# Scan bursts, block turns and weight sums at other places of a Mamba-2 scan with an ELU feed-forward

## The chip, the cores and the metric

The kernel runs on one NeuronCore of a Trainium2 chip. The metric is the device time of one execution in microseconds, as the median of six runs. The profile is one execution, taken by the hardware profiler.

## The reference

The inputs are x [4, 8, 768, 32], a decay a [4, 8, 768], B and C [4, 8, 768, 16], and two weight matrices w_in [256, 2048] and w_out [2048, 256] that come as 64-bit floats. A state-space scan runs for each batch and head over the sequence; its result y, with the heads side by side, is the input of a feed-forward block with an ELU.

```python
for c in range(nc):                      # chunks of the sequence
    cum = np.cumsum(log_a[:, :, sl], axis=-1)
    L = np.exp(cum[..., :, None] - cum[..., None, :]) * causal
    M = np.einsum('bhin,bhjn->bhij', Cc, Bc) * L
    y[:, :, sl] = M @ xc + np.einsum('bhin,bhnd->bhid', Cc, state) * np.exp(cum)[..., None]
    state = decay_full * state + sum_j (B_j * decay_from_j) x_j
...
x = y.transpose(0, 2, 1, 3).reshape(3072, 256)
h = x @ w_in
g = np.where(h > 0, h, np.exp(np.minimum(h, 0)) - 1)
out = g @ w_out                          # [3072, 256]
```

## The kernel before

The 3072 tokens are cut into 12 blocks of 256 (n = 0 to 11); a block is one of the three parts of one batch's sequence, with all eight heads. Within a block the scan works on chunks of 64 tokens. The order of the instructions on every engine is written out by hand in one program; the loops at the end of the function decide what follows what. All DMAs of the part concerned here are issued by SyncE (SP), in the order of the program.

**The scan of a block** has these steps:
- `load_bc(n)` (L106) and `load_x(n)` (L132) fetch B, C and x. For n > 5 B and C are fetched in a layout "of squares" (L121) for VectorE's transposes, and B once more by tokens (L113, tile b_tok). For n up to 5 B and C come by tokens alone (L129). `spread_cum` and `spread_exp` fetch the sums of the decays.
- The turn of B and C: blocks up to 5 use `turn(n)` (L383): four TensorE transposes into two PSUM tiles (L389), a copy to SBUF by ScalarE (L393) and the masked C by VectorE (L396), then `turn_exp(n)` (L400, L404). From block 6 on `turn_part(n, part)` is used: parts 0 and 1 are one VectorE transpose each (L413), part 2 the masked C (L421), part 3 the `turn_exp` (L404).
- `scaled(n)` (L374, on GpSimd) makes B times a decay, tile sc; `decay` makes L on ScalarE and GpSimd.
- `scores` (L501), `sums` (L531), `across` (L576) and `inside` (L595) are bursts of many small TensorE products: `scores` 32 for each block, `sums` 24 or 32, `across` up to 32 and `inside` 64. `weigh` (L510) multiplies the scores by L on VectorE, and `states` (L548, L553) carries the state; its tiles Sx are read by `across`. The end of a block is `inside(across(n), n)`, whose results are copied to yT.

**The feed-forward block** takes two forms. Blocks 0 to 3 use plain products: `l1(n, i)` (L625) makes a slice h, `elu` (L638, L645, L647) makes g, `l2(n, i)` (L746) adds to the output. Blocks 4 to 11 are handled in pairs (n, n+1) with seven products in place of eight at both matrices. `front`, `mid` and `back` (products at L697, sums by VectorE at L714, L722 and L730) make h for a pair; `second(n)` is a generator whose every step issues two products (L807) for the output of the pair. It lags by two blocks: while n = 4 is in `front`, `second(2)` runs. Its sums of g are made on GpSimd (L762, L774).

In a pair `front` writes the PSUM tile c2, `front_sums` (L714) reads both halves of it on VectorE into the tile u_sum, and the second product of `mid` then adds to a half of c2 that `front_sums` has read.

The sums of the weights for the seven products are made in place by `sum_weights` (four operations at L673), for w_out on VectorE and for w_in on GpSimd, one of eight slices at a time. `more_sums(i)` does slice i of both, and one sum of g on VectorE (L774). In the kernel before, slices 0 to 5 are made while n = 3, and slices 6 and 7 are spread over the first steps of n = 4 (`left`).

**The order around the change.** For n = 2 and 3 there is a loop of eight steps i: `l2(n - 2, i)`, `l1(n, i)`, the elu, and `scan_ahead(n, i)`, which holds the scan steps of blocks that come later. For n = 4, 6, 8, 10 there is a loop of 16 half steps k. An even k has `front`, an elu and four steps of `second` (`l2s`); an odd k has `mid`, `back`, two elus and three steps of `second`. The scan of the next pair m = n + 2 is laid between them: `scores(m, m + 1)` at k = 9, `sums` at k = 10, `states` at k = 11. The table `ends` says at which step of which n the end of a pair of blocks (across, inside, and `sum_y` on GpSimd) is issued.

PSUM is one pool of seven tiles in rotation (ps_h, ps_g, ps_st, ps_y, ps_tb, ps_tc and every second ps_o), and one tile apart.

`idle_product(k)` (L229) is a product of zeros with k times 128 columns, issued three times at the start: twice ahead of the first data, once ahead of `weigh(0, 0)`.

Of the kernel before, what the change touches and what calls it, by code (L numbers as in the profile page):

```python
# [16 lines left out]
P = 128  # L17
# [11 lines left out]
def kernel(  # L29
# [76 lines left out]
    def load_bc(n, c_queue=nc.sync):  # L106
        b, g = place(n)
        st.setdefault(n, {})["bc"] = raw.tile([P, 2, 2, NH, N], F32, tag="bc", name="bc", bufs=2)
        if n > 5:
            st[n]["b"] = raw.tile([P, 2, NH, N], F32, tag="b", name="b_tok", bufs=2)  # L110
            for u in range(2):
                sl = slice((2 * g + u) * P, (2 * g + u + 1) * P)
                nc.sync.dma_start(  # L113
                    out=st[n]["b"][:, u], in_=B[b, :, sl, :].rearrange("h s n -> s h n"))


            squares = st[n]["bc"].rearrange("p k u h n -> p k (u h n)").rearrange(
                "p k (m r) -> p k m r", m=2)
            for k, src in enumerate((B, C)):
                for m in range(2):  # L120
                    nc.sync.dma_start(  # L121
                        out=squares[:, k, m],
                        in_=src[b, m:NH:2, g * BLK:(g + 1) * BLK, :].rearrange(
                            "q (c t) n -> q c (t n)", t=8))
            return
        for u in range(2):
            sl = slice((2 * g + u) * P, (2 * g + u + 1) * P)
            for k, src in enumerate((B, C)):
                (nc.sync, c_queue)[k].dma_start(  # L129
                    out=st[n]["bc"][:, k, u], in_=src[b, :, sl, :].rearrange("h s n -> s h n"))  # L130
# [98 lines left out]

    def idle_product(k):  # L230

        nc.tensor.matmul(  # L232
            out=ps_idle[:, 0:k], lhsT=idle, rhs=idle.unsqueeze(1).to_broadcast([P, k, P]),
            start=True, stop=True)

    idle_product(4)
    idle_product(3)
# [136 lines left out]
    def scaled(n, eng):  # L374

        s = st[n]
        s["sc"] = sc = att.tile([P, 2, NH, N], F32, tag="sc", name="sc", bufs=2)
        factor = eb0[:, :, NH * n:NH * (n + 1)] if n < 2 else eb[:, :, rows_of(n)]
        eng.tensor_tensor(
            out=sc, in0=s["b"] if n > 5 else s["bc"][:, 0],  # L380
            in1=factor.unsqueeze(3).to_broadcast([P, 2, NH, N]), op=ALU.mult)

    def turn(n):  # L383
# [16 lines left out]
    def turn_exp(n, eng=nc.vector):  # L400

        s = st[n]
        s["cts"] = att.tile([P, 2, P], F32, tag="cts", name="cts", bufs=2)
        eng.tensor_tensor(out=s["cts"], in0=s.pop("ct"), in1=s["ec"], op=ALU.mult)  # L404
# [258 lines left out]
    def sum_weights(eng, a, s, i):  # L663
        for step in weight_steps(eng, a, s, i):
            step()
# [337 lines left out]
            elu()  # L1003


    ends = {(3, 13): (4, 5), (4, 13): (6, 7), (6, 13): (8, 9), (8, 12): (10, 11)}

    def end_of_two(n, step):
        ns = ends.get((n, step))
# [9 lines left out]
    def scan_ahead(n, i):  # L1019


        m = n + 2 + n % 2
        if 4 < m < NP and n % 2 == 1 and i in (4, 5):
            spread_cum(m + i - 4)
        m = n + 2 - n % 2
        if 4 <= m < NP and n % 2 == 0:
            if i < 2:
                if m == 4:
                    load_bc(m + i)
                spread_exp(m + i)  # L1030
            if i == 2:
                if m == 4:
                    spread_cum(5)
                load_x(m)
                load_x(m + 1)
            for k in (i,) if m == 4 else (i, i + 1) if i % 2 == 0 else ():
                if k >= 2:
                    decay(m + k // 6, (k - 2) % 4)
            if m == 4 and i in (5, 7):
                turn(m + i // 7)  # L1040
                turn_exp(m + i // 7)
        if n % 2 == 1 and i in (1, 3) and n + 3 + i // 2 < NP:
            load_bc(n + 3 + i // 2)
        if n == 3 and i > 3 and i < 7:
            turn_part(6, i - 4)
        if 4 <= m < NP and n % 2 == 1:
            if i == 0:
                scaled(m, nc.gpsimd)
                scaled(m + 1, nc.gpsimd)
            for k in (i,) if m == 4 else (i, i + 1) if i % 2 == 0 else ():  # L1050
                if k < 2:
                    decay(m + 1, k + 2)
            if i == 2 and m == 4:
                scores(m, m + 1)
                sums(m, m + 1)
                for q in range(4):
                    weigh(m, q)
                    weigh(m + 1, q)
                states(m)
                states(m + 1)  # L1060
# [21 lines left out]
    for n in (2, 3):  # L1082
        for i in range(8):
            l2(n - 2, i)
            if todo < len(pieces):
                w_take(todo, nc.vector)
            end_of_two(n, 2 * i)
            l1(n, i)
            if todo < len(pieces):
                w_give(todo)  # L1090
                w_load(todo + 6)
                todo += 1
            while lag:
                elu()
            if n == 2:
                if i < 2:
                    decay(3, 2 * i)
                    decay(3, 2 * i + 1)
                if i == 1:
                    scaled(3, nc.gpsimd)  # L1100
                    turn(3)
                    turn_exp(3)
                if i == 2:
                    scores(3)
                    for q in range(4):
                        weigh(3, q)
                if i == 4:
                    sums(3)
                    states(3)
                if i == 6:  # L1110
                    inside(across(3), 3)
            else:
                if i == 0:
                    s_in[:], s_out[:] = weight_sums(), weight_sums()
                elif i < 7:
                    more_sums(i - 1)
            scan_ahead(n, i)
            end_of_two(n, 2 * i + 1)
    sum_t2(2, 0)
    left = (step for i in (6, 7) for step in weight_steps(nc.vector, a_out, s_out, i))  # L1120

    for n in range(4, NP, 2):
        m = n + 2 if n + 2 < NP else None
        steps = second(n - 2)

        def l2s(count):
            for _ in range(count):
                next(steps)

        def next_elu():  # L1130
            if lag:
                at = lag[0][:2]
                elu()
                if at[0] % 2:
                    sum_t1(at[0] - 1, at[1])

        for k in range(16):
            i = k // 2
            if k % 2 == 0:
                if m and i == 5:  # L1140
                    l2s(4)
                    next_elu()
                    weigh_two(m, 1)
                    sums(m, m + 1)
                    front(n, i)
                    weigh_two(m, 2)
                    front_sums(n, i)
                    weigh_two(m, 3)
                else:
                    front(n, i)  # L1150
                    front_sums(n, i)
                    next_elu()
                    l2s(2)
                    end_of_two(n, k)
                    l2s(2)
            elif m and i == 5:
                l2s(1)
                mid(n, i)
                begin_elu()
                states(m)  # L1160
                l2s(2)
                back(n, i)
                next_elu()
                states(m + 1)
                begin_elu()
            else:
                mid(n, i)
                if i == 0 and n > 4:
                    store(n - 4, 0)
                    store(n - 4, 1)  # L1170
                begin_elu()
                turn_step(n, k, False)
                l2s(2)
                back(n, i)
                next_elu()
                begin_elu()
                turn_step(n, k, True)
                if n == 4 and i < 4:
                    for _ in range(2):
                        next(left)()  # L1180
                    if i < 2:
                        sum_weights(nc.gpsimd, a_in, s_in, 6 + i)
                        sum_t1(2, 6 + i)
                l2s(1)
            if m:
                scan_ahead(n + k // 8, k % 8)
                if k == 9:
                    scores(m, m + 1)
                    weigh_two(m, 0)
                if k % 2:  # L1190
                    end_of_two(n, k)
        for _ in steps:
            pass
# [44 lines left out]
```

## Time and profile before

| what | value |
|---|---|
| median of 6 runs | 362.88 us (362.57 to 364.58) |
| profiled execution, its own time | 364.58 us |
| its span, first to last instruction | 362.9 us |
| mean granted TensorE clock | 0.994 |
| TensorE matmuls busy | 353.6 us, 97% |
| VectorE, ScalarE, GpSimd busy | 66%, 55%, 64% |
| DMA moved | 26.09 MB in 85,845 packets |

The stretches of the span, by TensorE's timeline: 0 to 53.8 us blocks 0 and 1 with the conversion of the weights; 53.8 to 85.5 us n = 2; 85.5 to 117.7 us n = 3; from 117.7 us the pairs n = 4, 6, 8 and 10; from 334 us the last pair's second product alone. A busy time of TensorE includes overlaps of matmuls that follow each other; the difference of two starts in the timeline tells what one costs. A gap is shown with what ended it; "issue" stands where the profile shows nothing that the engine waited for.

### The profile page before, as it was taken

Reading aid. Unit: us, or ns where it says so; the run is one execution under the profiler, and the core shown is the slowest. Engines: PE = TensorE matmul, PEld = TensorE weight load, DVE = VectorE, ACT = ScalarE, POOL = GpSimd, SP = SyncE. Lnnn points to the kernel's source line nnn. Section 1 sums busy time; section 2 is a strip of 40 time slices with the busy share of each in tenths; the row PEclk is TensorE's granted clock in tenths of the full one; section 3 lists DMA queues with packets and bytes.
Section 4 is the critical chain, followed back from the end, with each engine's and each line's share of the span. In section 5 each row is a group of like instructions: output and inputs, shape, how many; then the busy total and the mean of one; then the engine's idle time right before and its main releaser. Section 6 shows DMA issues by size and latency. Waiting matters only on the chain.

```text
span 362.9 us, 9921 instructions
## 1 busy us (share of the span) xinstructions
PE 353.6 (97%) x3954; PEld 316.0 (87%) x3954; DVE 240.4 (66%) x495; ACT 201.0 (55%) x493; POOL 231.9 (64%) x368
## 2 busy tenths in 40 slices
PE   8899999999999999999999999999989999999995
PEld 5578878888888998989999989999979999999995
DVE  3989987982699778674777574777563456556212
ACT  4758969767435676545576545576534443535000
POOL 4553543673557997879386969386966445455983
PEclk9999999999999999999999999999998999999999
DMA  8977999552350500146500146500000100000001
GB/s 147 223 191 144 239 312 176 85 94 45 71 119 15 106 0 3 18 97 139 101 0 2 18 100 135 103 3 0 2 2 4 58 2 1 0 2 31 30 2 58
DMA packets 85845, 26.09 MB, mean 72 GB/s; under 512 B 63848, under 2 KB 81704, under 8 KB 85800
## 3 DMA queue, kind: packets, MB, share of 16 engines
q1 hardware_dynamic: 83624, 25.27, 31.8%
q8 instruction: 31, 0.51, 0.6%
q10 hardware_dynamic: 2176, 0.20, 0.5%
q14 instruction: 14, 0.11, 0.1%
HBM read 22.12 MB, written 3.34 MB: 70 GB/s over the span
## 4 chain that ended last, share of the span: by engine, by line
PE 83%; DVE 5%; POOL 4%; ACT 2%; issue 2%; DMA 2%; SPq 1%; POOLq 0%
PE ps_o L807 32%; PE ps_h L697 25%; PE ps_h L625 10%; PE ps_o L746 8%; PE ps_y L595 2%; DMA w<-in_moe_w_in_dram 2%; POOL g L762 2%; SPq L129 1%; PE ps_g L501 1%; PE ps_y L576 1%; PE ps_st L531 1%; DVE mag L200 1%; PE ps_idle L232 1%; DVE sgn L192 1%; POOL g L774 1%
## 5 line engine op out<-in xcount | busy, mean ns | idle before, releaser
L638 ACT ACTIVATE e<-ps_h 128x512 f32<-128x512 f32 x96 | 57.1, 594 | 92.2 <-DVE ps_h L722 45.4
L807 PEld LDWEIGHTS ps_o<-w_out,g 128*128 128x128 f32 x640 | 80.3, 192 | 3.3 <-issue 0.5
L807 PE MATMUL ps_o<-w_out,g 128*128 128x128 f32 x640 | 81.4, 275 | 0.0
L647 DVE SCALAR_TENSOR_TENSOR g<-e,ps_h 128x512 f32<-128x512 f32 x96 | 65.1, 679 | 15.8 <-ACT e L645 15.3
L625 PE MATMUL ps_h<-yT,w_in 128*128 128x256 f32 x256 | 60.7, 383 | 2.2 <-ACT w_in L181 1.1
L645 ACT ACTIVATE e<-e 128x512 f32<-128x512 f32 x96 | 60.9, 635 | 2.0
L774 POOL TENSOR_TENSOR g<-g 128x256 f32<-128x256 f32 x34 | 25.2, 742 | 55.4 <-DVE g L647 55.4
L625 PEld LDWEIGHTS ps_h<-yT,w_in 128*128 128x128 f32 x256 | 47.7, 190 | 10.5 <-POOL w_in L217 3.2
L807 PE MATMUL ps_o<-w_sum,g 128*128 128x128 f32 x320 | 43.8, 279 | 0.0
L807 PEld LDWEIGHTS ps_o<-w_sum,g 128*128 128x128 f32 x320 | 42.0, 195 | 1.5
L481 ACT ACTIVATE L<-L,ncum 128x64 f32<-128x64 f32 x160 | 41.0, 337 | 0.0
L697 PE MATMUL ps_h<-y_sum,w_sum 128*128 128x256 f32 x128 | 39.0, 387 | 0.5 <-DVE u_sum L714 0.5
L697 PE MATMUL ps_h<-yT,w_in 128*128 128x256 f32 x128 | 39.2, 388 | 0.0
L697 PE MATMUL ps_h<-y_sum,w_in 128*128 128x256 f32 x128 | 38.1, 380 | 0.0
L730 DVE TENSOR_TENSOR ps_h<-ps_h,u_sum 128x512 f32<-128x512 f32 x32 | 22.4, 699 | 23.6 <-PE ps_h L697 23.5
L486 POOL TENSOR_SCALAR_AFFINE_SELECT L<-L 64x512 f32<-64x512 f32 x40 | 27.8, 696 | 13.1 <-ACT L L481 11.8
L722 DVE TENSOR_TENSOR ps_h<-ps_h,u_sum 128x256 f32<-128x256 f32 x32 | 13.8, 432 | 30.1 <-PE ps_h L697 29.7
L714 DVE TENSOR_TENSOR u_sum<-ps_h,u_sum 128x512 f32<-128x512 f32 x32 | 22.0, 688 | 13.3 <-PE ps_h L697 7.9
L746 PE MATMUL ps_o<-w_out,g 128*128 128x256 f32 x128 | 30.8, 383 | 0.0
L762 POOL TENSOR_TENSOR t<-g 128x256 f32<-128x256 f32 x40 | 29.4, 766 | 0.3
L762 POOL TENSOR_TENSOR g<-g,t 128x256 f32<-128x256 f32 x40 | 28.8, 752 | 0.2
L697 PEld LDWEIGHTS ps_h<-y_sum,w_sum 128*128 128x128 f32 x128 | 24.2, 192 | 5.5 <-DVE u_sum L714 2.3
(111 smaller groups left out, 539.7 us busy)
## 6 DMA issues: line engine op xcount, KB each, us to landing
L<-flat SPq DMA_DIRECT2D x20, 256.0 KB, 6.1
w<-in_moe_w_in_dram SPq DMA_DIRECT2D x8, 512.0 KB
w<-in_moe_w_out_dram SPq DMA_DIRECT2D x8, 512.0 KB, 9.9
xr<-in_x_dram SPq DMA_DIRECT2D x24, 128.0 KB, 2.8
out_dram<-c_sum SPq DMA_DIRECT2D x10, 256.0 KB
bc<-in_B_dram SPq DMA_DIRECT2D x24, 64.0 KB, 5.9
bc<-in_C_dram SPq DMA_DIRECT2D x22, 64.0 KB
ec<-flat_exp SPq DMA_DIRECT2D x9, 128.0 KB
```

The source lines that it names most:

```text
L481: nc.scalar.activation(L[:, h, u], L[:, h, u], ACT.Exp, bias=ncum[:, u, row:row + 1])
L486: nc.gpsimd.affine_select(out=part, in_=part, pattern=[[0, 4], [0, 2], [1, Q]], compare_op=ALU.is_ge, fill=0.0, base=0, channel_multiplier=-1)
L625: nc.tensor.matmul(out=ps[:, j], lhsT=w_in[:, k, m * P:(m + 1) * P], rhs=yT[n // 2][:, k, n % 2].rearrange("p u i -> p (u i)"), start=(k = ...
L638: nc.scalar.activation(begun[0], lag[0][2], ACT.Relu, scale=-1.0)
L645: nc.scalar.activation(e, e, ACT.Exp, scale=-1.0)
L647: nc.vector.scalar_tensor_tensor(out=g_of[n, i], in0=e, scalar=1.0, in1=ps, op0=ALU.subtract, op1=ALU.max)
L697: nc.tensor.matmul(out=out, lhsT=lhsT, rhs=rhs, start=first, stop=True, skip_group_check=True)
L730: nc.vector.tensor_tensor(out=c2, in0=c2, in1=u[:, 0:2], op=ALU.add)
L746: nc.tensor.matmul(out=o_of[n][:, ts], lhsT=g_of[n, j][:, m % 2, ts * P:(ts + 1) * P], rhs=w_out[:, m], start=(m == 0 and ts == 0), stop=( ...
L762: nc.gpsimd.tensor_tensor(out=out, in0=in0, in1=in1, op=ALU.subtract)
L774: eng.tensor_tensor(out=b12, in0=b12, in1=b11, op=ALU.subtract)
L807: nc.tensor.matmul(out=ps[:, ts], lhsT=b[:, ts * P:(ts + 1) * P], rhs=a[:, i], start=(i == chunk[0] and ts == 0), stop=(i == chunk[-1]), s ...
```

## The change

- Blocks 4 and 5 are loaded in squares and by tokens, as blocks from 6 on were, and turned by `turn_part` in place of `turn`. The parts lie in the steps i = 3 to 7 of n = 2, and i = 0, 2 and 3 of n = 3.
- Slice 6 of the weight sums is made by `more_sums(6)` at the last step of n = 3, and its sum of g goes to VectorE with it. `left` holds slice 7 alone, one VectorE operation in each of four steps.
- The end of the blocks 10 and 11 is issued at k = 13 of n = 8 in place of k = 12.
- In n = 4, 6 and 8 one step of `second` is taken from the end of k = 9, ahead of `scores`, and put ahead of `mid` at k = 11.
- `idle_product(k)` issues k products of 128 columns in place of one with k times 128.

```diff
     def load_bc(n, c_queue=nc.sync):
...
-        if n > 5:
+        if n > 3:
             st[n]["b"] = raw.tile([P, 2, NH, N], F32, tag="b", name="b_tok", bufs=2)
...
     def idle_product(k):
-        nc.tensor.matmul(
-            out=ps_idle[:, 0:k], lhsT=idle, rhs=idle.unsqueeze(1).to_broadcast([P, k, P]),
-            start=True, stop=True)
+        for j in range(k):
+            nc.tensor.matmul(out=ps_idle[:, j], lhsT=idle, rhs=idle, start=True, stop=True)
...
-            out=sc, in0=s["b"] if n > 5 else s["bc"][:, 0],
+            out=sc, in0=s["b"] if n > 3 else s["bc"][:, 0],
...
-    ends = {(3, 13): (4, 5), (4, 13): (6, 7), (6, 13): (8, 9), (8, 12): (10, 11)}
+    ends = {(3, 13): (4, 5), (4, 13): (6, 7), (6, 13): (8, 9), (8, 13): (10, 11)}
...
     # scan_ahead
-            if m == 4 and i in (5, 7):
-                turn(m + i // 7)
-                turn_exp(m + i // 7)
+            if m == 4 and i > 2:
+                turn_part(m + i // 6, i % 3)
...
-        if n == 3 and i > 3 and i < 7:
+        if n == 3 and i == 0:
+            turn_part(5, 2)
+        if n == 3 and i in (2, 3):
+            turn_part(i + 2, 3)
+        if n == 3 and i in (4, 5, 6):
             turn_part(6, i - 4)
...
     # n = 3, step i
                 if i == 0:
                     s_in[:], s_out[:] = weight_sums(), weight_sums()
-                elif i < 7:
+                else:
                     more_sums(i - 1)
...
-    left = (step for i in (6, 7) for step in weight_steps(nc.vector, a_out, s_out, i))
+    left = weight_steps(nc.vector, a_out, s_out, 7)
...
     # n = 4, 6, 8, 10, half step k
             elif m and i == 5:
-                l2s(1)
+                l2s(2)
                 mid(n, i)
...
                 if n == 4 and i < 4:
-                    for _ in range(2):
-                        next(left)()
-                    if i < 2:
-                        sum_weights(nc.gpsimd, a_in, s_in, 6 + i)
-                        sum_t1(2, 6 + i)
-                l2s(1)
+                    next(left)()
+                    if i == 0:
+                        sum_weights(nc.gpsimd, a_in, s_in, 7)
+                        sum_t1(2, 7)
+                if not m or i != 4:
+                    l2s(1)
```

## The prediction

> **What bounds the kernel now.** First the page's busy line, then TensorE's timeline and its list of waits, then VectorE's timeline where the change puts work.
>
> ```profile
> PE 353.6 (97%) x3954; PEld 316.0 (87%) x3954; DVE 240.4 (66%) x495; ACT 201.0 (55%) x493; POOL 231.9 (64%) x368
> q8 instruction: 31, 0.51, 0.6%
> ```
>
> TensorE is the bound: from 28 us on it is dense, so each matmul removed or stall added there moves the end one for one, unless it meets one of the few gaps. The second line becomes important: 0.51 MB in 31 packets are 16 KB each, TensorE's own instructions.
>
> ```profile
> 52.70 1.24 PE L625 MATMUL ps_h<-yT,w_in 128*128 128x256 f32 x5 [0.24 <-issue]
> 76.33 0.38 PE L389 MATMUL ps_tb<-ident,bc 128*128 128x128 f32 x2
> 76.55 0.38 PE L389 MATMUL ps_tc<-ident,bc 128*128 128x128 f32 x2
> 76.77 1.89 PE L746 MATMUL ps_o<-w_out,g 128*128 128x256 f32 x8
> 121.18 0.59 PE L697 MATMUL ps_h<-y_sum,w_sum 128*128 128x256 f32 x2
> 140.30 0.70 PE L697 MATMUL ps_h<-y_sum,w_sum 128*128 128x256 f32 x2 [0.52 <-DVE u_sum L714]
> 268.55 1.24 PE L576 MATMUL ps_y<-cts,Sx 32*64 32x64 f32 x64
> 269.71 0.79 PE L595 MATMUL ps_y<-M,xr 64*32 64x64 f32 x56
> 272.00 0.96 PE L595 MATMUL ps_y<-M,xr 64*32 64x64 f32 x72 [1.50 <-issue]
> ```
>
> Columns are start, duration, operation, idle before. See: four transposes take 0.44 us of the stream (76.33 to 76.77); one wait of 0.52 us for VectorE's u_sum; and two gaps with releaser "issue", at 52.7 and in the middle of the scan burst of blocks 10 and 11 at 270.5.
>
> **The gaps are instruction fetches.** Numbering TensorE's records (loads, matmuls, semaphore events) in order of start, the work resumes after the gaps at records 1473 and 6593: 5,120 apart, 20 times 256. The Trainium skill, "Runtime: NRT & Kernel Launch", section "Instruction fetch mechanics", says that instructions come in 16 KiB blocks of 256, the next fetched while the present one runs, at a cost mostly hidden. The packet size and the 5,120 agree; "hidden" does not hold here. Block starts are thus records 193+256k. In the packet list the two fetches start 1.79 and 1.37 us after TensorE enters a block without lead (52.70, 272.00), and the next block runs 2.5 to 2.7 us after the packet starts (50.16 to 52.70; 269.29 to 272.00). Under heavy DMA load, early, the first part is longer: 3.0 us after 9.09, 4.3 after 23.09, 3.9 after 46.24. A scan burst eats a block in 1.5 us, a plain stretch in 14 or more. Taking 2.6 us to arrival, the slack at every block start works out as positive except at the two gaps; the smallest others are 0.85 us at record 449, 0.96 at 961 and 1.93 at 5569.
>
> **The clock.**
>
> ```profile
> 271.00:272.00 1.00, 0.00 (x0) 0.00 (x0) 0.00 (x0) 0.00 (x0) 0.92 (x2) 1.00 0.00 0
> 274.00:275.00 1.00, 1.00 (x6) 0.91 (x6) 0.00 (x0) 0.29 (x1) 0.57 (x1) 0.50 0.00 0
> ```
>
> The third value from the end is the granted clock: after the gap it is half for 3.4 us. "TensorE: Matmul & The Clock Gate", Part 1, describes half rate after low activity, in windows of 3,413 ns; the trace agrees. The loss is 1.7 us. The profiled execution took 364.58 us (span 362.9 and 1.7 around it), the median is 362.88: exactly this window less. So I add up against 362.88, and assume the burst's stall itself is in every run.
>
> **VectorE ahead of the first pair.**
>
> ```profile
> 116.72 0.94 DVE L774 TENSOR_TENSOR g<-g 128x256 f32<-128x256 f32 x1
> 117.59 1.21 DVE L421 TENSOR_TENSOR ctm<-bct,hmask 128x512 f32<-128x512 f32 x1
> 119.16 0.69 DVE L647 SCALAR_TENSOR_TENSOR g<-e,ps_h 128x512 f32<-128x512 f32 x1 [0.36 <-PE ps_h L697]
> 119.76 0.69 DVE L714 TENSOR_TENSOR u_sum<-ps_h,u_sum 128x512 f32<-128x512 f32 x1
> ```
>
> VectorE has no idle from 99.85 to 118.8; the first pair's u_sum ends at 120.45, and TensorE's second product of mid(4,0), which overwrites what u_sum reads, starts at 121.18: slack 0.73 us.
>
> **Part by part.**
>
> 1. *Blocks 4 and 5 turned by VectorE.* TensorE loses two times four transposes: 0.44 + 0.43 us, -0.9. ScalarE loses two copies (0.35 each), off the path. VectorE loses 2 x (0.68+0.42), gains four 32-row transposes (L413, 0.64 each, 0.49 from start to start), two masks (L421, 0.7 to 1.2) and two cts (L404, 0.43). The first two transposes enter 62 to 80 us, where VectorE is dense and w_out pieces 14 and 15 end on GpSimd 0.5 and 1.5 us before l2 takes them: 0 to +0.5. I take 0, since I expect TensorE later there (part 4). PSUM gains four free tiles. SP issues six DMAs instead of four per block, two at 0.58 each more; it idles from 62.7 to 66.7, and the load is used 4 us or more after its landing (median 5.9 after issue). B of block 6 now waits for sc(4) at 89.7 instead of leaving at 85.2; its first use is at 110: nothing.
>
> 2. *more_sums(6) in the last step of block 3.* GpSimd's four L673 (2.1 us) now precede t2, which TensorE needs at 128.2 and which would end at 123.6: nothing. VectorE's four L673 and one L774 stand ahead of u_sum of the first pair. Such groups take 1.85, 2.27, 2.28, 2.54 and 2.92 us in the trace, mean 2.4; the spread is VectorE and GpSimd excluding each other ("SBUF — State Buffer", section "SBUF: two separate sides": a lock held for the whole instruction; the L673 of 0.26 and 0.76 us agree). The two cts put in at block 3 cost 2 x 0.34 less 0.36 of idle: +0.3. So u_sum ends at 120.45 + 2.7 = 123.15 against 121.18: **+2.0** (1.4 to 2.7). In return each step in n = 4 has one sum fewer, u_sum at 139.57 comes some 0.6 us sooner, and the 0.52 wait goes: -0.5.
>
> 3. *Last burst from step 12 to 13.* At 268.55 the burst waited for Sx, made until 269.02, and then for its block. A whole burst takes 2.42 us elsewhere (218.35 to 220.77) and 4.41 here: **-2.0** if both waits go. In its new place some 57 records later the Sx are old and the entered block was asked for some 6 us before. The block after it begins about 46 records past the burst, which take some 3.1 us, against 2.8 until it arrives: bounds 0 to +0.7, I take 0. y_sum has two steps left, as after the bursts of the other pairs. The l2 step moved past scores, three times, makes scores 0.44 us earlier and gives mid more cover (0.14 us wait at 155.6 each); but sums then meets a PSUM tile freed at 152.26 by L647: 0, bounds ±0.4.
>
> 4. *Idle products as single matmuls.* Each fp32 matmul is two loads and two matmuls; ten instead of three add 28 records (20 before record 134). Their own time is set by columns: 128-column matmuls in L807 follow each other in 0.111 us, hardly more than wide ones: 0. But every later record moves 28 on against the block starts, until the turns take 16 back.
>    - Record 449 falls into the end of inside(0), reached at 12.05; asked for at 8.8, fetched at 11.85, there at 14.45. The first l1 starts at 15.0, not 13.27. It absorbs its own wait for w_in; about 0.9 is left at 23.
>    - Record 961 is now the head of l1 of block 1, due at 28.05. Asked for while sums(1) runs at 23.9, fetched 4.3 later, there at 30.8 (30.0 without the delay before). From here TensorE is dense: +2.5 (1.9 to 3.0).
>    - Record 1473 falls 22 records inside the burst of block 2: 1.5 us of stall instead of 0.4: +0.9 (-0.4 to +1.2).
>
>    Together **+3.4**, bounds -0.4 (no stall appears, the old 0.4 goes) to +4.2.
>
> Sum: -0.9 + 2.0 - 0.5 - 2.0 + 3.4 = +2.0, hence 364.9 us.
>
> **Rivals.**
> - *Fetches keep ahead (faster).* If the early fetches do not depend on the 28 records as I think, because the blocks are asked for earlier than I infer, part 4 is about 0. For it: early latencies are read with unknown lead. Against it: only two starts have no slack, and just these stall. Sum -1.4: 361.5. The sign turns where part 4 costs less than 1.4 us.
> - *u_sum not late.* If VectorE catches up before 117 us, part 2 gives -0.5 alone: 362.9. Against it: no idle for 19 us.
> - *A cold window too.* An early stall after a burst resembles the one at 270.5 and may halve the clock for 3.4 us: +1.7, 366.6.
> - *The burst moved in vain.* If it straddles another late block, its 2.0 stays: 366.9.
>
> **How the numbers follow.** Main case 0.50 (own range 363.6 to 366.3), fetches ahead 0.25 (360.6 to 362.6), u_sum not late 0.11 (362.0 to 364), the last two 0.14 (366 to 368). About 0.3%, or 1.1 us, is what can be told from no change: under 361.8 lies most of the second case, 0.22; between, parts of three cases, 0.19; over 364.0, 0.59. Range 360.9 to 367.2.
>
> **What would show it.** Right: "issue" gaps near 12, 28 and 54 us; l1 of block 1 at about 30.5; a wait of about 2 us for L714 at mid(4,0); none at the last burst, clock full after it. Wrong: the dense stretch starting at 28, or no wait at mid(4,0).

## The result, and the profile after

| what | before | after |
|---|---|---|
| median, measured side by side | 363.23 us (72 runs, 361.5 to 366.28) | 363.92 us (35 runs, 361.29 to 366.84) |
| ratio of after to before | | 1.0013, 95% interval 0.9999 to 1.0026 |
| profiled execution, its own time | 364.58 us | 365.76 us |
| its span | 362.9 us | 364.0 us |
| its mean granted TensorE clock | 0.994 | 0.986 |

The change made no difference that can be told from none. The forecast was slower by 2.0 us; the measured 364 us lie inside its range. The two profiles end 1.1 us apart, but they are not alike: matmul by matmul the changed kernel lies 4.2 us behind after the first stall, 6.2 us behind after the second (at 123 us of before), and wins most of it back at the last burst. Lines past L233 have a number one lower than before.

The page's busy line and the line of the granted clock (40 slices of the span, tenths of full speed):

```profile
PE 353.5 (97%) x3960; PEld 318.7 (88%) x3960; DVE 241.8 (66%) x500; ACT 200.5 (55%) x491; POOL 231.3 (64%) x367
PEclk9789999999999989999999999999999999999999
```

TensorE is as busy as before, with six matmuls more. The clock dips in the slices 2, 3 and 15 (of 9.1 us each). TensorE's longest waits (total, times, longest, in us):

```profile
PE ps_y L594 <- issue: 2.8, 1, 2.8
PE ps_h L696 <- DVE u_sum L713: 2.5, 1, 2.5
```

These are the two new waits that the prediction named. TensorE's timeline (start, duration, operation, idle before and what ended it) places them. First two lines of before, then the kernel after:

```profile
11.12 1.01 PE L595 MATMUL ps_y<-M,xr 64*32 64x64 f32 x64
28.08 10.63 PE L625 MATMUL ps_h<-yT,w_in 128*128 128x256 f32 x48
```

```profile
11.23 0.99 PE L594 MATMUL ps_y<-M,xr 64*32 64x64 f32 x60
15.02 0.42 PE L594 MATMUL ps_y<-M,xr 64*32 64x64 f32 x4 [2.79 <-issue]
...
31.44 4.80 PE L624 MATMUL ps_h<-yT,w_in 128*128 128x256 f32 x21
...
53.53 1.22 PE L594 MATMUL ps_y<-M,xr 64*32 64x64 f32 x64
...
122.67 0.60 PE L696 MATMUL ps_h<-yT,w_in 128*128 128x256 f32 x2
125.79 0.67 PE L696 MATMUL ps_h<-y_sum,w_sum 128*128 128x256 f32 x2 [2.53 <-DVE u_sum L713]
...
278.12 1.51 PE L594 MATMUL ps_y<-M,xr 64*32 64x64 f32 x128
```

The burst `inside(0)` stops four matmuls before its end; the work resumes at record 449. The long l1 of block 1 starts at 31.44, against 28.08 before. In the burst of block 2 at 53.53, record 1473 starts 0.34 us after the record before it (0.13 us of it idle). At `mid(4,0)` the second product waits 2.53 us. The last burst, which took 4.41 us, has no gap: `inside` of blocks 10 and 11 is one piece of 1.51 us. The 0.52 us wait that stood at 140.30 is gone.

The windows of the trace (the granted clock is the third value from the end) show what follows each of the two stalls:

```profile
16.00:17.00 1.00, 1.00 (x4) 0.82 (x3) 0.56 (x2) 1.00 (x3) 0.50 (x1) 0.50 0.82 276
21.00:22.00 1.00, 1.00 (x19) 0.85 (x19) 0.62 (x2) 0.33 (x2) 0.34 (x1) 1.00 0.47 122
127.00:128.00 1.00, 1.00 (x6) 1.00 (x5) 0.48 (x1) 0.97 (x2) 1.00 (x2) 0.50 0.00 0
130.00:131.00 1.00, 1.00 (x7) 0.92 (x6) 1.00 (x3) 0.59 (x2) 1.00 (x2) 1.00 0.00 0
```

Half rate holds from 14.0 to 20.8 us (two windows of 3.413 us on end) and from 126.6 to 130.0 (one). Each such window can cost up to 1.7 us. In before's profile there is one, after the gap in the last burst.

**The same split over all runs.** Every run lists its mean granted clock, and one window of 3.41 us at half rate lowers it by about 0.005. So the clock of a run tells how many windows it had. Of 35 runs of after 3 had none (361.4 us in the median), 7 had one (362.8), 19 had two or nearly so (364.0) and 6 three (365.6). Of the 107 runs of the kernel before that were made beside the experiments, 78 had none (some 362.9 us) and 29 had one or, twice, two. The clock tells only how many windows a run had; where they lie is seen in the profiled run alone. **At full clock, then, the change is a gain of about 1.4 us (three runs); the windows of half clock, which in the profile follow its two new stalls, take it back.**

### The profile page after: what moved, and what is told of

Read it like the earlier page. It is cut to its first block, busy times and chain, and to the rows that moved or that the text cites. A ratio compares the mean times of both kernels' runs of the same rounds, so it can differ in the third digit from the quotient of the medians.

```text
span 364.0 us, 9939 instructions
## 1 busy us (share of the span) xinstructions
PE 353.5 (97%) x3960; PEld 318.7 (88%) x3960; DVE 241.8 (66%) x500; ACT 200.5 (55%) x491; POOL 231.3 (64%) x367
## 4 chain that ended last, share of the span: by engine, by line
PE 95%; DVE 2%; issue 1%; POOL 0%; POOLq 0%
PE ps_o L806 34%; PE ps_h L696 27%; PE ps_h L624 16%; PE ps_o L745 8%; PE ps_y L594 3%; PE ps_g L500 2%; PE ps_y L575 2%; PE ps_st L530 1%; PE ps_idle L233 1%; PE ps_x L451 1%; PE ps_x L440 0%; PE ps_x L459 0%; POOL w_in L217 0%; DVE w_sum L672 0%; PE ps_tb L388 0%
## 5 line engine op out<-in xcount | busy, mean ns | idle before, releaser
L773 POOL TENSOR_TENSOR g<-g 128x256 f32<-128x256 f32 x33 | 24.0, 728 | 57.7 <-DVE g L646 57.6
L624 PEld LDWEIGHTS ps_h<-yT,w_in 128*128 128x128 f32 x256 | 49.1, 194 | 7.8 <-POOL w_in L217 0.2
L806 PE MATMUL ps_o<-w_sum,g 128*128 128x128 f32 x320 | 42.9, 275 | 0.0
L806 PEld LDWEIGHTS ps_o<-w_sum,g 128*128 128x128 f32 x320 | 41.1, 192 | 1.2
L696 PE MATMUL ps_h<-y_sum,w_sum 128*128 128x256 f32 x128 | 38.2, 380 | 2.5 <-DVE u_sum L713 2.5
L485 POOL TENSOR_SCALAR_AFFINE_SELECT L<-L 64x512 f32<-64x512 f32 x40 | 28.9, 722 | 11.1 <-ACT L L480 9.7
```

The source lines that it names most:

```text
L485: nc.gpsimd.affine_select(out=part, in_=part, pattern=[[0, 4], [0, 2], [1, Q]], compare_op=ALU.is_ge, fill=0.0, base=0, channel_multiplier=-1)
L624: nc.tensor.matmul(out=ps[:, j], lhsT=w_in[:, k, m * P:(m + 1) * P], rhs=yT[n // 2][:, k, n % 2].rearrange("p u i -> p (u i)"), start=(k = ...
L696: nc.tensor.matmul(out=out, lhsT=lhsT, rhs=rhs, start=first, stop=True, skip_group_check=True)
L773: eng.tensor_tensor(out=b12, in0=b12, in1=b11, op=ALU.subtract)
L806: nc.tensor.matmul(out=ps[:, ts], lhsT=b[:, ts * P:(ts + 1) * P], rhs=a[:, i], start=(i == chunk[0] and ts == 0), stop=(i == chunk[-1]), s ...
```

## The experiments

All times are medians, with the ratio to the kernel before on the same chip. "No window" means runs at a mean clock of 0.997 or more.

Theory: TensorE's instructions come in blocks of 256, and a scan burst that reaches a block start too early stalls; VectorE's queue makes u_sum late; a stall draws half clock. Rivals: the split costs by its own matmuls; GpSimd's sums are what is late; the parts do as the prediction sized them, without windows.

### The idle split alone

```diff
-        nc.tensor.matmul(
-            out=ps_idle[:, 0:k], lhsT=idle, rhs=idle.unsqueeze(1).to_broadcast([P, k, P]),
-            start=True, stop=True)
+        for j in range(k):
+            nc.tensor.matmul(out=ps_idle[:, j], lhsT=idle, rhs=idle, start=True, stop=True)
```

> The kernel before with the idle products alone split into single matmuls (28 more TensorE records, nothing else). Fetch theory: record 449 falls into the end of inside(0), so a gap of releaser issue of 2 to 3 us stands near 12 us, l1 of block 0 starts at about 15 instead of 13.3, and what is left of it at l1 of block 1 (28.1 us before) is 1 to 3 us; the burst of blocks 10 and 11 still stalls, since 28 records move block start 6593 from record 243 of the burst to record 215, still inside. Time +1.0 to +2.5 us. Rival (the split itself costs nothing and the order of the stream is all the same): no gap at 12 us, time within 0.5 us.

Measured: 364.42 us (360.43 to 366.43), ratio 1.0003 (0.9974 to 1.0033). TensorE's timeline:

```profile
15.08 0.43 PE L594 MATMUL ps_y<-M,xr 64*32 64x64 f32 x4 [3.07 <-issue]
...
55.58 0.33 PE L594 MATMUL ps_y<-M,xr 64*32 64x64 f32 x11 [1.46 <-issue]
...
273.60 1.51 PE L594 MATMUL ps_y<-M,xr 64*32 64x64 f32 x128
```

The split makes two stalls, at records 449 and 1473, and removes a third, against my forecast. The block start 6593 still lies in the last burst, at 274.02, as expected, but its block is not late: the packet came at 267.71, 6.3 us before it was needed, in place of 2.7 us in before (269.29 for 272.00). The block that TensorE runs meanwhile is entered 28 records sooner, 3.5 us ahead of `across` in place of 0.9. With this stall gone the median is that of before, and not the 1.0 to 2.5 us more that I expected. Twelve of 14 runs have windows (364.7 us); the two without took 360.4 and 361.1.

### The change without the idle split

The edit is the one above, undone in the changed kernel.

> The changed kernel with the idle products as one matmul each, as before. Fetch theory: no issue gap near 12 us, l1 of block 1 back at about 28.1 us, the later stall of about 2.5 us at mid(4,0) stays. Time 1 to 2.5 us under the changed kernel, so 362 or less, and faster than before by some 1 us. Rival (the early stall is absorbed before TensorE becomes dense): no change against the changed kernel.

Measured: 362.77 us, 1.2 us under the changed kernel, ratio 0.9973 (0.9955 to 0.9991); without a window 361.4 (10 runs), with one or more 363.1 (12 runs).

```profile
12.90 2.49 PE L625 MATMUL ps_h<-yT,w_in 128*128 128x256 f32 x8 [1.13 <-POOL w_in L217]
...
123.53 0.67 PE L697 MATMUL ps_h<-y_sum,w_sum 128*128 128x256 f32 x2 [2.52 <-DVE u_sum L714]
```

No fetch gap at 12 us, only the first l1's wait for its weights; the wait for u_sum stays.

### The change without the moved weight sums

```diff
-                else:
+                elif i < 7:
                     more_sums(i - 1)
...
-    left = weight_steps(nc.vector, a_out, s_out, 7)
+    left = (step for i in (6, 7) for step in weight_steps(nc.vector, a_out, s_out, i))
...
                 if n == 4 and i < 4:
-                    next(left)()
-                    if i == 0:
-                        sum_weights(nc.gpsimd, a_in, s_in, 7)
-                        sum_t1(2, 7)
+                    for _ in range(2):
+                        next(left)()
+                    if i < 2:
+                        sum_weights(nc.gpsimd, a_in, s_in, 6 + i)
+                        sum_t1(2, 6 + i)
```

> The changed kernel with the weight sums of slice 6 back in the first steps of n = 4 (left, as before). Theory of VectorE's queue: the wait of 2.5 us for u_sum at mid(4,0) goes, a wait of 0 to 0.5 us at mid(4,3) comes back; the gap at 12 us stays. Time 1.5 to 2.5 us under the changed kernel, more where the stall also cost a cold clock window. Rival (the wait is due to the two cts of blocks 4 and 5 put into n = 3, not to the sums): the wait at mid(4,0) stays above 1.5 us.

Measured: 361.3 us, 2.6 us under the changed kernel, ratio 0.9934 (0.9911 to 0.9958); no window 359.4 (4 runs), with 361.5 (12 runs).

```profile
14.43 0.30 PE L594 MATMUL ps_y<-M,xr 64*32 64x64 f32 x4 [2.79 <-issue]
...
122.26 0.59 PE L696 MATMUL ps_h<-y_sum,w_sum 128*128 128x256 f32 x2
```

The stall in `inside(0)` is that of the changed kernel; `mid(4,0)` runs through.

### Turns, burst and moved step: neither split nor moved sums

Both edits undone in the changed kernel.

> The changed kernel without the split idle products and without the moved weight sums: what remains is the turn of blocks 4 and 5 by VectorE, the last burst at step 13 and the moved l2 step. Theory: neither the gap at 12 us nor the wait at mid(4,0) nor the stall in the last burst; -0.8 for the transposes, -2.0 for the burst, -0.3 to -0.9 for the moved step: 359.5 to 360.5 us if before is at 363.2, ratio 0.990 to 0.993. Rival (gains on a dense TensorE are given back by cold clock windows elsewhere): 362 or more.

Measured: **359.18 us** (358.54 to 359.97), ratio 0.9883 (0.9853 to 0.9913); no run has a window. This beats both kernels. Against it, the sums cost 362.77 - 359.18 = 3.6 us, of which 2.3 without windows (361.4); the split costs 361.3 - 359.18 = 2.1, but 0.2 without windows (359.4).

### The last burst alone

```diff
-    ends = {(3, 13): (4, 5), (4, 13): (6, 7), (6, 13): (8, 9), (8, 12): (10, 11)}
+    ends = {(3, 13): (4, 5), (4, 13): (6, 7), (6, 13): (8, 9), (8, 13): (10, 11)}
```

> The kernel before with one edit: the end of blocks 10 and 11 issued at k = 13 of n = 8. The prediction's step gives -2.0 us (about 361.2 us beside a before of 363.2): the burst's gap and its wait for Sx go, nothing else. The rival that I now hold likelier: the gap of 1.5 us usually brings a window of half clock with it in the runs of the kernel before, so that -2.0 and part of 1.7 us go together: -2.2 to -3.7 us, median about 360.5, with a spread of under 2 us. If the burst straddles another late block in its new place, the gap shows there and the gain is under 0.5 us.

Measured: 360.69 us (359.47 to 361.93), ratio 0.9939 (0.9921 to 0.9957): -2.4 us. No run of 12 has a window; of the 35 of the kernel before beside it six have one (365.0), and the other 29 stand at 362.9. So my expectation that the window comes with most runs of the kernel before was wrong: -2.2 us is the gap and the wait for Sx, the rest the windows of a few runs. The burst itself:

```profile
272.07 0.91 PE L576 MATMUL ps_y<-cts,Sx 32*64 32x64 f32 x64
272.91 1.51 PE L595 MATMUL ps_y<-M,xr 64*32 64x64 f32 x128
```

### The turns added to it

The edits of `load_bc`, `scaled` and `scan_ahead`, on top of the last kernel.

> The kernel before with the turns of blocks 4 and 5 by VectorE and the last burst at k = 13, without the moved step of second. It sizes the first and the moved step apart. By the traces: turns -0.5 to -0.8 us beside 360.7 us of the burst alone, so 360.0; the moved step then is worth the rest to 359.2, three times 0.25 us. Rival (the prediction's own sizes: turns -0.9, moved step 0): 359.3, the same as with the moved step.

Measured: 360.72 us (359.35 to 361.77), ratio 0.9918 (0.9886 to 0.9949), where I expected 360.0 and the rival said 359.3. The intervals of this kernel, of the burst alone and of the kernel with the moved step overlap, so the times don't size the two parts; the traces do. Matmul by matmul against the burst alone, its lag goes from +0.25 us at 52 us to -0.19 after block 4's transposes and -0.56 after block 5's: -0.8. But half of this is lost again at `mid(4,5)`, where the burst alone has no such wait and the lag goes back to -0.16:

```profile
154.90 0.70 PE L697 MATMUL ps_h<-y_sum,w_sum 128*128 128x256 f32 x2 [0.33 <-DVE u_sum L714]
```

The moved step takes this wait away, and has an effect at every `mid(n,5)`. TensorE's timeline there at n = 6, in this kernel without it:

```profile
208.60 0.60 PE L697 MATMUL ps_h<-yT,w_in 128*128 128x256 f32 x2
209.18 0.70 PE L697 MATMUL ps_h<-y_sum,w_sum 128*128 128x256 f32 x2
```

And in the kernel of 359.18 us, with it:

```profile
208.69 0.60 PE L697 MATMUL ps_h<-yT,w_in 128*128 128x256 f32 x2
209.12 0.59 PE L697 MATMUL ps_h<-y_sum,w_sum 128*128 128x256 f32 x2
```

From start to start 0.58 us without and 0.43 with the four more matmuls of cover: the wait of 0.15 is gone, and the slower first matmul after it (0.09) too. That is 0.24 us at n = 6 and the same at n = 8. At n = 4 it is 0.44 against the kernel without the moved step, but only 0.1 against the kernel before, which has no wait of 0.33 us there. So the moved step is worth some 0.6 us against the kernel before, with the turns' 0.8 in full, and 0.9 on top of the turns.

### Which engine's sums make u_sum late

Neither split nor moved VectorE sums, but GpSimd's sums of slice 6 early:

```diff
                 elif i < 7:
                     more_sums(i - 1)
+                else:
+                    sum_weights(nc.gpsimd, a_in, s_in, 6)
...
-                    if i < 2:
-                        sum_weights(nc.gpsimd, a_in, s_in, 6 + i)
-                        sum_t1(2, 6 + i)
+                    if i == 0:
+                        sum_weights(nc.gpsimd, a_in, s_in, 7)
+                    if i < 2:
+                        sum_t1(2, 6 + i)
```

> The kernel without the idle split and with VectorE's sums of slice 6 left in the steps of n = 4 (turns, burst and the step of second as in the change), but with GpSimd's four sums of slice 6 made at the last step of n = 3. It tells VectorE's queue from GpSimd's load. Theory (five VectorE operations queued ahead of u_sum): no wait at mid(4,0), 359.2 us as without any moved sums, within 0.4. Rival (the two engines hold each other up, or GpSimd's part is what is late): a wait of over 1 us at mid(4,0) or at its neighbours, 360.5 us or more.

Measured: 359.5 us (358.35 to 360.79), ratio 0.9917 (0.9886 to 0.9948). TensorE's timeline has no wait at `mid(4,0)`:

```profile
119.21 0.59 PE L697 MATMUL ps_h<-y_sum,w_sum 128*128 128x256 f32 x2
```

It is VectorE's queue. In the changed kernel VectorE's timeline there reads:

```profile
121.71 0.48 DVE L672 TENSOR_TENSOR w_sum<-w_out 128x128 f32<-128x128 f32 x1
122.22 0.50 DVE L672 TENSOR_TENSOR w_out<-w_out 128x128 f32<-128x128 f32 x1
122.75 0.70 DVE L672 TENSOR_TENSOR w_sum<-w_out 128x128 f32<-128x128 f32 x1
123.49 0.69 DVE L672 TENSOR_TENSOR w_sum<-w_out,w_sum 128x128 f32<-128x128 f32 x1
124.11 0.94 DVE L773 TENSOR_TENSOR g<-g 128x256 f32<-128x256 f32 x1
124.97 0.68 DVE L713 TENSOR_TENSOR u_sum<-ps_h,u_sum 128x512 f32<-128x512 f32 x1
```

From 121.71 to 124.97 the five operations take 3.26 us, all ahead of u_sum.

### A smaller dose of the split

From here on the base is the kernel of 359.18 us. Only the last idle product is split, 8 records more:

```diff
     scores(0)
-    idle_product(3)
+    for j in range(3):
+        nc.tensor.matmul(out=ps_idle[:, j], lhsT=idle, rhs=idle, start=True, stop=True)
```

> The kernel with turns, burst and the step of second as in the change, weight sums as before, and only the last of the three idle products split: 8 records more instead of 28. Theory (blocks of 256 records): the start of the second block, which was reached at 14.74 us, moves 8 records back into l1 of block 0, four matmuls of about 0.3 us each: reached near 13.5, there at 14.6, so a gap of 0.7 to 1.4 us in the middle of l1(0), not of 3; and the later block start at record 1473 falls at the end of the burst of block 2: a gap of 1.0 to 1.6 us there, in place of 0.5. In all +0.8 to +2.0 us against 359.2, more if clock windows follow. Rival (the split costs by its own matmuls, or by how they keep the clock): no gap at these places, and the cost in proportion to the matmuls added, 2 of 7: +0.6 us.

Measured: 360.71 us (359.91 to 361.92), ratio 0.9941 (0.9918 to 0.9964), +1.5. Record 449 comes at 14.42 in the middle of l1(0), 0.59 us after the start of the record before it, with TensorE idle for 0.11 (in the base it was reached at 14.74, behind l1(0), without a gap); record 1473 stops the last matmul of the burst of block 2:

```profile
53.85 0.21 PE L595 MATMUL ps_y<-M,xr 64*32 64x64 f32 x1 [1.59 <-issue]
```

The places are those that counting records gives; the early gap is smaller than the 0.7 to 1.4 us expected, the later one at the upper end of 1.0 to 1.6.

### 256 records more

Two idle products are split as in the change (20 records more), and the third (4 records) is replaced by 60 small products of zeros (240 records): 20 + 236 = 256 records more than the base.

```diff
-    idle_product(4)
-    idle_product(3)
+    for j in range(60):
+        nc.tensor.matmul(
+            out=ps_idle[0:64, j % 4, 0:32], lhsT=idle[0:64, 0:64], rhs=idle[0:64, 0:32],
+            start=True, stop=True)
+    for j in range(4):
+        nc.tensor.matmul(out=ps_idle[:, j], lhsT=idle, rhs=idle, start=True, stop=True)
...
     scores(0)
-    idle_product(3)
+    for j in range(3):
+        nc.tensor.matmul(out=ps_idle[:, j], lhsT=idle, rhs=idle, start=True, stop=True)
```

> The kernel with turns, burst and the step of second as in the change and weight sums as before, whose idle products of 4 and of 3 blocks are split, and which issues 60 small products of zeros (64x64 weights, 32 columns) at the start in place of the other idle product: 256 TensorE records more than without the split, none of which feeds an output. Theory (only the place of the work against block starts counts, and these repeat every 256): the gap of some 3 us at 12 us goes although the idle products are split; block starts lie where they lay before the split, with about 0.5 us of gap at 53 us; 359 to 360 us. One block more is fetched at the start: asked for near 2.5 us, it is there near 8 to 9, so that scores(0) may stall by up to 1 us. Rival (the split itself, or the number of records, costs): a gap of 2.5 us or more near 12 us remains, 361 us or more.

Measured: 371.73 us, ratio 1.0219 (1.0175 to 1.0263). The filler took 13.01 us, 0.11 us a matmul, and moved the whole start by 12 us; my size for it was wrong. The gap at the end of `inside(0)` is gone, but so late a start meets other transfers, so this alone shows little. A second form lets the small products lie on four column groups in turn:

```diff
+    for j in range(60):
+        v, q = j % 2, j % 4
+        nc.tensor.matmul(
+            out=ps_idle[32 * q:32 * q + 32, j % 4, 0:64], lhsT=idle[64 * v:64 * v + 64, 0:32],
+            rhs=idle[64 * v:64 * v + 64, 0:64], start=True, stop=True,
+            tile_position=(64 * v, 32 * q), skip_group_check=True)
...
```

> As the kernel with 60 small products of zeros at the start, but these products lie on four column groups of the array in turn (64 rows, 32 columns of weights, 64 columns moved), so that they overlap; those before did not, took 13 us and so moved the whole start. Expected: 3 to 6 us for the 120 matmuls, the scan of block 0 some 1 to 5 us later than without. Theory: no gap of more than 1 us near the first l1 though two idle products are split, since the block starts lie where they lay without the split; end 0.5 to 4 us after 359.2 by the later start alone. Rival (the split or the number of records costs): a gap of 2.5 us or more at the end of inside(0) or in the first l1, and that much more time.

Measured: 361.07 us (360.02 to 362.32), ratio 0.9953 (0.9935 to 0.9972). The filler takes 3.43 us. TensorE's timeline at the end of block 0:

```profile
11.80 1.01 PE L601 MATMUL ps_y<-M,xr 64*32 64x64 f32 x64
13.94 2.49 PE L631 MATMUL ps_h<-yT,w_in 128*128 128x256 f32 x8 [1.14 <-POOL w_in L217]
```

`inside(0)` is whole again, and the split is still there. The median is 1.9 us above the base: the start is some 1.5 us later (`across(0)` at 11.29 in place of 9.73), and four of eight runs have a window; the other four stand at 360.5. With 28 records more the burst stalls, with 256 more it does not: where the work lies against block starts, which repeat every 256 records, decides about this stall. The fetch itself did not change: the packet for record 449 came at 11.96 in the base and at 11.94 in the kernel without the moved sums, which stalls.

### No idle products, and one fewer

```diff
-    idle_product(4)
-    idle_product(3)
...
     scores(0)
-    idle_product(3)
```

> The kernel with turns, burst and the step of second as in the change, weight sums as before, and the three idle products left out (12 records fewer; they feed no output). Theory: all block starts come 12 records later in the work; record 449 stays in l1 of block 0 or the conversion with more lead, and record 1473 falls well inside l1 of block 2, about 1 us later than now, so that the gap of 0.54 us at 53 us goes: -0.3 to -0.6 us, 358.7. Rival (the idle products serve the clock): half rate at the start lasts longer, and the first scan bursts and l1 of block 0 run slower: +0.5 to +2 us.

Measured: 363.66 us (359.56 to 366.67), ratio 0.9987 (0.9961 to 1.0013): +4.5 against the base, where I expected -0.5. The gap at 53 us did go. But the first products now run slowly for longer (the first record of full clock is at 9.3 us in this profile, at 4.5 in the base's), and the burst of blocks 6 and 7 stalls at a block start:

```profile
8.17 0.63 PE L387 MATMUL ps_tc<-ident,bc 128*128 128x128 f32 x2
...
167.88 0.78 PE L593 MATMUL ps_y<-M,xr 64*32 64x64 f32 x55 [2.56 <-issue]
```

(The transposes take 0.38 in the base.) The base's burst lies across the same block start, record 4033, without a gap; the packet came at 159.16 there, 5.8 us before it was needed, and here at 165.14, when the block before was used up. Fifteen of 22 runs have windows; the seven without stand at 361.0, so that the slow start and the new gap are 1.8 us and the windows the rest (a run's mean clock does not count the slow start).

With only the last idle product left out:

```diff
     scores(0)
-    idle_product(3)
```

> The kernel with turns, burst and the step of second as in the change, weight sums as before, and only the last idle product (384 columns, ahead of across(0)) left out, 4 records fewer. Theory: across and inside of block 0 come 0.8 us sooner, and with them the first l1; record 1473 falls two matmuls later in l1 of block 2, and the gap of 0.54 us there shrinks to about 0.1: -0.3 to -1.0 us against 359.2. Rival 1 (it serves the clock, as all three together did): half rate for 3.4 us in some runs, +0.5 us or more in the median. Rival 2 (block starts 4 records later meet another burst, as twelve records did at 165 us): a new gap of 1 to 2.8 us at a burst.

Measured: 359.42 us (358.98 to 360.05), ratio 0.9883 (0.9842 to 0.9925): the same as the base, and not the 0.3 to 1.0 us less that I expected. The gap at 53 us is gone, but the 0.8 us gained at the start turn into a wait of 0.6 us for Sx ahead of across(0), and three of six runs have a window. These three are no slower than the others (359.41 and 359.44 us in the median); in the profiled one the window lies at 13.3 to 16.7 us.

## Why the prediction was wrong, step by step

| part | predicted | at full clock | median |
|---|---|---|---|
| 1, turns | -0.9 | -0.8 (traces) | |
| 2, weight sums | +1.5 | +2.3 (traces +1.9) | +3.6 |
| 3, last burst | -2.0 | -2.2 | -2.4 |
| 3, moved step of second | 0 (±0.4) | -0.6 (traces) | |
| 4, idle split | +3.4 | 0 to +0.2 | +2.1 |
| sum | +2.0 | -1.2 | +1.9 |

The column at full clock comes near to what was measured: -0.8 + 2.3 - 2.2 - 0.6 + 0.1 = -1.2, and after's three runs without a window stand at 361.4 against some 362.9. With the traces' values where there is no median, the last column gives -0.8 + 3.6 - 2.4 - 0.6 + 2.1 = +1.9, and the whole change shows +0.7. Most of the difference lies in the two parts that draw windows: added to the base one by one, sums and split cost 3.6 + 2.1 = 5.7 us, together 363.92 - 359.18 = 4.7; taken out of the whole change, the split is worth 1.2 and the sums 2.6. Why they cost less together is not shown. That the sum of the medians comes near to the forecast of +2.0 is luck: too much was said for the split and too little for the sums.

**Part 4 failed, in its second line.** It had record 961 stall the head of l1 of block 1 by 2.5 us, with the fetch of 4.3 us that one block of one profile took, and with TensorE dense from there on. Neither held. In the three profiles with the whole split (the change, the split alone, the change without the moved sums) the packet of this block came 1.4, 2.2 and 2.7 us after TensorE entered the block before, and record 961 started 0.26, 0.26 and 0.77 us after the record before it. That l1 of block 1 started at 31.4, near the 30.5 named as a sign, was no proof of this step: the 3.4 us come from the first gap and from the two windows of half clock after it. I had written that such latencies were "read with unknown lead" and yet took the longest one at its face value. The first line was right in place and size (resumed at 15.02 where 14.45 was said), and waits for w_in that were there anyway (1.14, 0.18 and 0.42 us in the profiles without the split) take in a part of the stall, as was said. But the rest of it is taken in too, because TensorE is not dense near 43 us. The kernel of 359.18 us waits there for ScalarE and VectorE:

```profile
42.59 1.51 PE L501 MATMUL ps_g<-ctm,bct 32*64 32x128 f32 x32 [0.33 <-ACT L L481]
44.52 1.99 PE L625 MATMUL ps_h<-yT,w_in 128*128 128x256 f32 x8 [0.42 <-DVE g L647]
```

The change without the moved sums, with stall and one window, is 3.0 us behind it at the head of l1 of block 1, 1.3 at 44.5, and 1.7 at the end, which is the window alone. So at full clock nothing is left of the stall. At record 1473 the gap was up to 1.5 us in different profiles, about as bounded.

What part 4 costs instead is what I had put aside as a rival with little chance, **a cold window too**. Its price was about right (1.7 us; in five kernels the medians with none and with one window are 1.3 to 2.1 apart, but in the kernel with one idle product fewer not at all), its frequency wrong: 12 of 14 runs with the split alone, 12 of 16 without the moved sums. "TensorE: Matmul & The Clock Gate", Part 1, of the Trainium skill speaks of half rate after low activity in windows of 3,413 ns; the trace shows the windows' length, and with a stall of some 3 us in a scan burst 24 of 30 runs had one or two of them.

**Part 2 was right in its mechanism and mis-sized.** The wait stands where it was said, ended by what was said, and the wait at 140.30 went. The five VectorE operations took 3.26 us, not 2.4, more than any of the five groups of before, whose 2.92 was the upper bound. Hence 2.53 us of wait where 2.0 was said. And 12 of 22 runs without the split have a window; the profile of the changed kernel shows one right after this wait.

**Part 3 was right** in the burst: -2.2 where -2.0 was said, and the block start in it was fetched early, as said (at 269.62 for 278.29 in the changed kernel). The gain fits the assumption that the gap is in the other runs of before too, which no trace shows. That the median of before is almost free of its window was right as well (29 of 107 runs have one). The moved step was costed at nothing because `sums` might meet a tile that is not free. That it gives mid more cover for its wait of 0.14 us was in the text; I set it against a loss that no trace shows, and so missed 0.6 us.

**Part 1 was right** in its size, -0.8 where -0.9 was said, but half of it comes to the end only together with the moved step, which the prediction costed apart.

The rival "fetches keep ahead" came near to the full-clock time (361.5), for another reason: the fetches do not keep ahead, the stall is hidden.

## What to carry to other kernels

A gap that the profile ends with "issue" in the middle of a burst of small matmuls is worth a count of instruction records: any edit anywhere ahead of it, even products that feed nothing, can move it to another place or away, and so a gain or loss by it says little about the edit itself. The count tells where a stall can be; whether one comes is told by when the block's packet came. Price a stall of TensorE twice, once for the idle time, which a wait nearby may already cover, and once for the half-rate window that it may draw, and read from each run's mean clock how often it does. Before work is moved to the last step ahead of a hand-over, list what stands in that engine's queue at that moment; here five short sums fitted everywhere but there.

## What the runs showed of the hardware that was not expected

- **How often half clock comes with a stall.** A gap of 2.8 to 3.1 us in the small matmuls of `inside(0)`: 24 of 30 runs without the moved sums. A wait of 2.5 us between large products: 12 of 22. The gap of 1.5 us in the last burst: 29 of 107 (each gap is known from the profiled run). In the kernels with none of them (the burst alone, with turns, with the moved step, with GpSimd's sums early): 0 of 33. It is not the length alone: the 1.6 us gap at 53 us in the smaller dose drew none in 8 runs, and three of six and four of eight runs of two kernels without such a gap (one idle product fewer; 256 records more) have a window. What decides between runs of one kernel stays open.
- **The lead of an instruction fetch changes.** The packet of the block after the one that TensorE enters came from 2.4 us ahead of the entry (at 161.60 in the base) to 2.96 us behind it (at 162.18, no idle products), in the same plain stretch of the program; the second made the gap of 2.56 us. Wherever the work stalled for a block, it resumed 2.3 to 2.7 us after the packet's start. The last burst shows the same: record 6593 lies in it in every kernel here but the two with 256 records more, and it stalls only in before, where the packet came 2.7 us ahead of need in place of 6.3 to 8.7. What sets the lead was not found, and so counting records tells where a stall is possible, but not whether it comes or how long it is. "Runtime: NRT & Kernel Launch", section "Instruction fetch mechanics", of the Trainium skill calls the cost of such a crossing mostly hidden; here it was between 0 and 3.1 us.
- **Small products of zeros on one place of the array follow each other slowly**: 120 matmuls took 13.01 us on one tile (64x64 weights, 32 columns; 0.108 us each), and 3.43 us on four column groups in turn (64x32 weights, 64 columns; 0.029 us each), both ahead of the first record of full clock.
